# Where a gate's preparation, its placements and the first expert tile's transposes stand in an attention loop

## The chip, the cores and the metric

The kernel runs on one core of a Trainium2 chip. The metric is the time of one execution on the device in microseconds (us). The core has a matrix engine (TensorE, in rows PE, its weight loads PEld), a vector engine (VectorE, DVE), a scalar engine (ScalarE, ACT), a general engine (GpSimd, POOL) and SyncE (SP), which here only starts transfers. Each engine works off its own instructions in the order in which they are written, and waits for the others through semaphores. TensorE writes its results into PSUM, from which ScalarE and VectorE copy them away.

## What is computed

Three layers follow one another: a gated linear attention over 4 sequences of 768 rows with 8 heads of 48, a mixture of 8 experts (each row goes to the one expert with the largest logit), and a gated feed-forward layer. The inputs of the part that matters here are q, k, v, the forget logits f, the modality id of each row, the gate's weights and one bias per modality and expert.

```python
f = 1.0 / (1.0 + np.exp(-f_logit))
for t in range(S):
    state = f[:, :, t, :, None] * state + np.einsum('bhd,bhe->bhde', k[:, :, t], v[:, :, t])
    y[:, :, t] = np.einsum('bhd,bhde->bhe', q[:, :, t], state)
...
logits = x @ w_gate + modality_bias[modality_id]
e_idx = np.argmax(logits, axis=1)
for e in range(E):
    mask = e_idx == e
    h = np.maximum(x[mask] @ w1[e], 0.0)
    out[mask] = gate_w[mask, None] * (h @ w2[e])
...
return (silu * val @ w_out).astype(np.float32)
```

## The kernel before

**The loop.** The attention runs over 24 tiles of 128 rows (6 chunks of 4 sequences) in a pipeline of 32 steps, written out by hand in `attention_fast`; within `manual_schedule` each engine keeps the order of the text. A tile t passes p0 at step t-1, p1 at t+1, p2 at t+2, p3 at t+3 and p4 at t+4.

- p0: VectorE clamps f (line 104), ScalarE takes Exp and Ln and casts the high part lh, GpSimd subtracts for the low part ll (line 114).
- p1: TensorE forms the running sums cum (lines 123 and 124) in the PSUM tile pm. VectorE clamps them into bc (line 128), ScalarE makes em and ep, VectorE kp = k em (line 133), GpSimd qp = q ep (line 134). SP then copies the last row of ep into dd (line 137).
- p2: TensorE transposes kp into the PSUM bank pk and qp into pq (line 151); ScalarE copies them to kt and qt (line 153). Each bank holds one tile at a time.
- p3: TensorE multiplies kt and qt into pa (line 162), VectorE masks the result into am (line 165), in two halves.
- p4: TensorE adds the products of the state (line 175, from the second chunk on) and of am with v (line 177) in py; ScalarE copies py to xs. VectorE updates gm and the state (lines 182 to 196), TensorE forms the state's increment pu (line 187), GpSimd scales the state.

**The gate.** Tiles are gated in groups of 4, 4, 2, 3, 3, 2, 2, 1, 1, 1 and 1. A tile's xs is transposed at step t+5 (`early`, px on TensorE, xt on ScalarE) and multiplied with the gate's weights at t+6 (`logits`). At the last tile of a group, VectorE adds the bias (lg, line 413) and `route` finds the expert in five short operations at step t+6. `ranks` and `place` follow at step t+7: `place` has one operation per tile (line 472) and six more (lines 475 to 486), all on VectorE, and gives each row its place among its expert's rows. `send` writes one tile per step to DRAM (xo on ScalarE, an indirect transfer on GpSimd's queue). A step's order on the queues is: loads, p4, logits, ranks, p3, p2, early, place and route taking turns, p1, p0, share, send, and last what the expert layer has put into slot 2 of the step.

**The gate's preparation** (`Gate.fill`) is a generator in two parts. The first, at step 3, starts three loads on SP's queue: the weights, the biases and the modality ids (mi, line 368). The second, at step 5, has eight VectorE operations (lines 371 to 394), of which the first reads mi, and three GpSimd iotas. In the same step `Plan.setup` issues eleven more GpSimd instructions: nine iotas and two memsets.

**The first expert tile.** From step 17 on the loop also prepares the first tile of 512 rows of the expert with the most rows. `Experts.early` keeps a table of calls by step and slot; f there is 17. VectorE finds the expert at the end of step 17 (`plan.first`, lines 603 to 614). Gathers follow in steps 19 and 20 in slot 1, weight loads and their casts (line 758 on ScalarE, line 760 on VectorE) from step 18 on in slot 2. The rows are turned in steps 22, 23 and 24 (`turn`, slot 2): four transposes of TensorE into a borrowed PSUM bank (line 776), a cast xh on ScalarE (line 686) and a difference xl on VectorE (line 687). The bank is that of pq, so the next step's pq transposes wait until xl has read it. From step 25 on, TensorE multiplies for that tile between the last steps of the attention.

Of the kernel before, what the change touches and what calls it, by code (L numbers as in the profile page):

```python
# [7 lines left out]
F32 = mybir.dt.float32  # L8
# [9 lines left out]
P = 128  # L18
# [44 lines left out]
def attention_fast(tc, io, cst, ps, gate, plan, first):  # L63
    nc = tc.nc
    q, k, v, f = io
    ident, tri, mask4, onesc = cst["ident"], cst["tri"], cst["mask4"], cst["onesc"]
    gm = cst["gm"]
    with ExitStack() as ctx:
# [24 lines left out]
        def load(t, names="fkqv"):  # L93
            d = T.setdefault(t, {})
            for nm, a in zip("fkqv", (f, k, q, v)):
                if nm not in names:
                    continue
                x = ld.tile([P, H, D], F32, tag=nm, name=nm, bufs={"f": 3, "v": 7}.get(nm, 4))
                nc.sync.dma_start(x, src(a, t))
                d[nm] = x  # L100

        def p0(t):
            d = T[t]
            nc.vector.tensor_scalar_max(d["f"], d["f"], -LCLAMP)
            e = wk.tile([P, H * D], F32, tag="e", name="e")
            nc.scalar.activation(e, d["f"].rearrange("p h d -> p (h d)"), AF.Exp, scale=-1.0)
            nc.scalar.activation(e, e, AF.Ln, bias=onesc)
            if t == 0:
                d["l"] = e
                return  # L110
            lh = wk.tile([P, H * D], F32R, tag="lh", name="lh")
            nc.scalar.copy(lh, e)
            ll = wk.tile([P, H * D], F32R, tag="ll", name="ll")
            nc.gpsimd.tensor_tensor(out=ll, in0=e, in1=lh.bitcast(F32), op=ALU.subtract)
            d["l"] = lh, ll
# [84 lines left out]
        with tc.manual_schedule():  # L200
            for t, names in ((0, "fq"), (1, "f"), (0, "k"), (1, "q"), (1, "k"), (2, "f"), (0, "v"), (1, "v"), (2, "v")):
                load(t, names)
            p0(0)
            setup = gate.setup()
            for s in range(NTILE + 8):
                if s == 1:
                    blank()
                if s == 3:
                    next(setup)
                    nc.gpsimd.memset(sb, 0.0)  # L210
                if s == 5:
                    next(setup)
                    plan.setup()
                if s + 3 < NTILE:
                    load(s + 3, "f")
                if s + 2 < NTILE:
                    load(s + 2, "kqv" if s else "kq")
                first(s, 0)
                if 0 <= s - 4 < NTILE:
                    p4(s - 4)  # L220
                if s in TWICE:
                    gate.send(1)
                gate.logits(s - 6)
                gate.ranks(s - 7)
                first(s, 1)
                if 0 <= s - 3 < NTILE:
                    p3(s - 3)
                if 0 <= s - 2 < NTILE:
                    p2(s - 2)
                if 0 <= s - 5 < NTILE:  # L230
                    gate.early(s - 5, T.pop(s - 5)["xs"])
                gate.turns(gate.place(s - 7), gate.route(s - 6))
                if 0 <= s - 1 < NTILE:
                    p1(s - 1)
                if s + 1 < NTILE:
                    p0(s + 1)
                gate.share(s - 6)
                gate.send(1)
                first(s, 2)
            first(NTILE + 8, 0)  # L240
# [289 lines left out]
T1 = 512  # L530
# [159 lines left out]
class Experts:  # L690
# [18 lines left out]

    def lent(self, ps):  # L710

        self.pt = lambda: ps["q"].tile([P, T1], F32, tag="pq", name="pt")
        self.ph = lambda m: ps["ukq"[m % 3]].tile([P, T1], F32, tag="p" + "ukq"[m % 3], name="ph")

        def py():
            a = ps["a"].tile([P, 2, T1], F32, tag="pa", name="py")
            return [a[:, 0], a[:, 1], ps["y"].tile([P, T1], F32, tag="py", name="py2")]

        self.py = py
# [165 lines left out]
    def early(self, plan, ps, pm):  # L885

        d = {}
        w = [[] for _ in range(4)]
        h = {}

        def regs():
            plan.first(self.tc)
            d["e"] = self.pick(plan)

        def load(u):
            d["r", u] = self.load(d["e"], *divmod(u, 2))

        def halves(u):
            r = d.pop(("r", u), None)
            if r is None:  # L900
                w[u // 2].extend(next(d.pop(("h", u))))
            else:
                d["h", u] = self.halves(r, u % 2)
                next(d["h", u])

        def fetch():
            d["xr"] = self.xp.tile([P, T1 // P, RW], F32, tag="xr", name="xr", bufs=1)

        def gather(j):

            i = self.gather(plan.list0, d["xr"], j).ins
            self.tc.declare_no_dep(i, group=self.later, keep=d.setdefault("got", []), reason="no row of the list is among them")
            d["got"].append(i)
            self.tc.add_to_no_dep_group(self.later, i)

        def turn(kk):
            if kk == 0:
                d["x"] = self.split_x()
            self.turn(T1, d["xr"], d["x"], kk)

        def up(m):
            h[m] = self.up(T1, w[m // 2], d["x"], m)

        def down(m):
            if m == 0:
                d["py"] = self.py()
            self.down(T1, w[m // 2], h.pop(m), d["py"], m)

        def ahead():
            d["rg"] = self.regs(plan, 0)  # L930
            T, e, ids, off = d["rg"]
            xr = self.fetch(T, ids)
            d["w"] = [self.weights(e, 0), [], []]
            for u in (2, 3, 4):
                d["n", u] = self.load(e, *divmod(u, 2))
            d["next"] = xr

        def second():
            for u in (2, 3):
                d["w"][1].extend(list(self.halves(d.pop(("n", u)), u % 2))[1])  # L940
            d["n", 5] = self.load(d["rg"][1], 2, 1)
            T, _, _, off = d["rg"]
            self.note(T, d["next"], off)

        def last():
            x = d["x"] = self.split_x()
            pt = [ps["x"].tile([P, T1], F32, tag="px", name="pt"), ps["q"].tile([P, T1], F32, tag="pq", name="pt"), pm]
            for j in range(T1 // P):
                for kk in range(3):
                    self.flip(pt[kk], d["next"], j, kk)  # L950
            for kk in range(3):
                self.part(T1, pt[kk], x, kk)
            for u in (4, 5):
                d["w"][2].extend(list(self.halves(d.pop(("n", u)), u % 2))[1])
            d["rg1"] = self.regs(plan, 1)
            d["rows1"] = self.rows(*d["rg1"][0:1], *d["rg1"][2:4])

        self.lent(ps)
        at = {}

        def on(s, x, fn, *args):
            at.setdefault((s, x), []).append(lambda: fn(*args))

        f = FIRST + 8
        on(f, 2, regs)
        on(f + 1, 2, fetch)
        for j in range(T1 // P):
            on(f + 2 + j // 2, 1, gather, j)
        on(f + 4, 2, self.noted, d)
        for kk in range(3):  # L970
            on(f + 5 + kk, 2, turn, kk)
        for u in range(6):
            on(f + 1 + u, 2, load, u)
            on(f + 2 + u, 2, halves, u)
            on(f + 3 + u, 2, halves, u)
        n = NTILE
        for u in (6, 7):
            on(n + 3 * (u - 6), 2, load, u)
        made = plan.make(self.tc)
        for m in range(3):  # L980
            on(n + 1 + m, 2, up, m)
        on(n + 3, 2, halves, 6)
        on(n + 4, 2, halves, 6)
        on(n + 4, 0, down, 0)
        on(n + 5, 0, up, 3)
        on(n + 6, 0, down, 1)
        on(n + 6, 2, next, made)
        on(n + 8, 0, up, 4)
        on(n + 8, 0, down, 2)
        on(n + 8, 0, halves, 7)  # L990
        on(n + 8, 0, up, 5)
        on(n + 8, 0, halves, 7)
        on(n + 8, 0, down, 3)
        on(n + 8, 0, up, 6)
        on(n + 8, 0, ahead)
        on(n + 8, 0, down, 4)
        on(n + 8, 0, up, 7)
        for m in (5, 6):
            on(n + 8, 0, down, m)
        on(n + 8, 0, second)  # L1000
        on(n + 8, 0, down, 7)
        on(n + 8, 0, last)
        on(n + 8, 0, next, made)
        self.begun = d

        def run(s, x):
            for fn in at.get((s, x), ()):
                fn()

        return run  # L1010
# [442 lines left out]
```

## Time and profile before

| what | value |
|---|---|
| time, median of 3 runs | 904.59 us (903.18 to 910.25) |
| the profiled execution | 905.4 us |
| its span, first to last instruction | 903.7 us |
| TensorE busy | 863.8 us (96%) |
| VectorE busy | 489.8 us (54%) |
| ScalarE busy | 364.8 us (40%) |
| GpSimd busy | 203.3 us (22%) |
| mean granted clock of TensorE | 0.980 |

The span is cut into engines' busy times; matmuls are pipelined and their ends modelled, so a busy TensorE is not one at its peak. The granted clock is a share of the full 2.4 GHz; 0.50 is its lower level of 1.2 GHz. A row of a timeline gives a start, a duration, engine, line and operation, the tiles written and read, and in brackets how long the engine had been idle before and what ended it. Steps are not marked in the trace; a step is taken to begin with the first product of p4 on TensorE, and the other engines run up to some microseconds behind it.

### The profile page before, as it was taken

To read this page: it belongs to the slowest core of one execution; us is meant where nothing else is said; L and a number is where in the kernel's file an instruction comes from. 1 tells how busy PE (TensorE), PEld (TensorE's weight loads), DVE (VectorE), ACT (ScalarE), POOL (GpSimd) and SP (SyncE) were. 2 spreads that over 40 slices of the span, in tenths; PEclk is the share of its full clock that TensorE was granted. 3 is DMA by queue.
4 is the path that set the end of the run, shared out by engine and by line. 5 is a ranking of instruction groups with operands and counts; after the bars stand their busy time and mean duration, and the time that the engine had idled before them with its cause. 6 is when DMAs were issued, how large, how long until landed. Compare 5 with 4: busy or idle time off the path is not lost.

```text
span 903.7 us, 13025 instructions
## 1 busy us (share of the span) xinstructions
PE 863.8 (96%) x4778; PEld 748.0 (83%) x4778; DVE 489.8 (54%) x1030; ACT 364.8 (40%) x661; POOL 203.3 (22%) x245
## 2 busy tenths in 40 slices
PE   5899999899999999998999999999999999999993
PEld 4899999887787888777887888888888888888883
DVE  3466887657767557534999736227225422532220
ACT  6577777643454545423534412222131231122121
POOL 4346577523233232101312300010010010001001
PEclk9799999899999999999999999999999999999997
DMA  9857667214564464453223100000000000000001
GB/s 183 143 110 146 133 162 192 78 65 148 156 195 142 128 196 132 96 164 83 70 71 101 40 1 0 1 36 1 1 36 0 1 36 1 1 1 35 1 1 38
DMA packets 145291, 70.59 MB, mean 78 GB/s; under 512 B 113040, under 2 KB 140176, under 8 KB 145216
## 3 DMA queue, kind: packets, MB, share of 16 engines
q1 hardware_dynamic: 140320, 55.18, 24.7%
q0 software_dynamic: 4896, 14.47, 4.6%
q8 instruction: 40, 0.66, 0.3%
q14 instruction: 35, 0.29, 0.1%
HBM read 60.08 MB, written 9.52 MB: 77 GB/s over the span
## 4 chain that ended last, share of the span: by engine, by line
issue 33%; PE 10%; DVE 6%; POOL 2%; ACT 1%; DMA 1%; SPq 0%; POOLq 0%; ACTq 0%
PE po L1292 4%; PE pg L1271 3%; PE pv L1271 3%; POOL out_dram L1303 2%; DVE q L1122 1%; DVE t L1120 1%; DVE t L1121 1%; DVE h L1283 1%; DMA r<-in_moe_w_out_dram 1%; DVE sg L1280 1%; DVE t L1119 0%; DVE hl L687 0%; DVE h L1282 0%; DVE rr L1231 0%; SPq L1104 0%
## 5 line engine op out<-in xcount | busy, mean ns | idle before, releaser
L1278 DVE TENSOR_TENSOR h<-sg,pv 128x512 f32<-128x512 f32 x60 | 41.2, 687 | 192.0 <-PE pv L1271 192.0
L1303 POOL DMA_INDIRECT out_dram<-o,cid x24 | 23.3, 970 | 363.4 <-ACT o L1301 360.8
L1277 ACT ACTIVATE sg<-pg 128x512 f32<-128x512 f32 x60 | 35.9, 598 | 147.2 <-PE pg L1271 147.2
L686 ACT CAST hh<-h 128x512 fp32r<-128x512 f32 x70 | 43.4, 621 | 124.6 <-DVE h L1278 113.3
L1271 PE MATMUL pv<-xh,w1h 128*128 128x512 f32 x216 | 85.6, 396 | 2.1 <-DVE xh L1244 2.1
L1271 PE MATMUL pg<-xh,w0h 128*128 128x512 f32 x216 | 86.1, 398 | 0.3 <-DVE sg L1280 0.3
L1271 PE MATMUL pg<-xh,w0l 128*128 128x512 f32 x216 | 85.7, 397 | 0.0
L1271 PE MATMUL pg<-xl,w0h 128*128 128x512 f32 x216 | 85.4, 397 | 0.4 <-DVE xl L687 0.4
L1271 PE MATMUL pv<-xh,w1l 128*128 128x512 f32 x216 | 85.1, 394 | 0.2 <-POOL w1l L1125 0.2
L1271 PE MATMUL pv<-xl,w1h 128*128 128x512 f32 x216 | 85.1, 395 | 0.0
L687 DVE TENSOR_TENSOR hl<-h,hh 128x512 fp32r<-128x512 f32 x70 | 48.4, 693 | 33.5 <-ACT hh L686 33.5
L1292 PE MATMUL po<-w2h,hh 128*128 128x384 f32 x280 | 62.2, 340 | 2.2 <-ACT hh L686 2.1
L760 DVE TENSOR_TENSOR l<-r,h 128x768 fp32r<-128x768 f32 x48 | 46.1, 965 | 31.9 <-ACT h L758 31.5
L1292 PE MATMUL po<-w2l,hh 128*128 128x384 f32 x280 | 62.3, 341 | 0.0
L1292 PE MATMUL po<-w2h,hl 128*128 128x384 f32 x280 | 62.1, 340 | 0.0
L799 PE MATMUL ph<-xh,h 128*128 128x512 f32 x144 | 58.4, 406 | 0.6 <-ACT xh L686 0.6
L1292 PEld LDWEIGHTS po<-w2h,hh 128*128 128x128 f32 x280 | 50.9, 188 | 8.8 <-ACT hh L686 3.5
L177 PE MATMUL py<-v,am 128*128 128x48 f32 x384 | 55.3, 272 | 2.8 <-issue 2.7
L799 PE MATMUL ph<-xh,l 128*128 128x512 f32 x144 | 57.9, 402 | 0.0
L799 PE MATMUL ph<-xl,h 128*128 128x512 f32 x144 | 57.5, 400 | 0.2 <-DVE xl L687 0.2
L177 PEld LDWEIGHTS py<-v,am 128*128 128x128 f32 x384 | 51.7, 198 | 3.3 <-issue 3.0
L1292 PEld LDWEIGHTS po<-w2l,hh 128*128 128x128 f32 x280 | 50.7, 190 | 0.0
(302 smaller groups left out, 1848.4 us busy)
## 6 DMA issues: line engine op xcount, KB each, us to landing
r<-in_moe_w_dram SPq DMA_DIRECT2D x48, 384.0 KB
f<-in_f_logit_dram SPq DMA_DIRECT2D x24, 192.0 KB
q<-in_q_dram SPq DMA_DIRECT2D x24, 192.0 KB
k<-in_k_dram SPq DMA_DIRECT2D x24, 192.0 KB
v<-in_v_dram SPq DMA_DIRECT2D x24, 192.0 KB
r<-in_moe_w_gate_dram SPq DMA_DIRECT2D x12, 384.0 KB
r<-in_moe_w_val_dram SPq DMA_DIRECT2D x12, 384.0 KB
r<-in_moe_w_out_dram SPq DMA_DIRECT2D x12, 384.0 KB
```

The lines of the kernel that those rows point to most:

```text
L177: nc.tensor.matmul(py[:, h, :], d["am"][:, h % 2, h // 2, :], d["v"][:, h, :], start=(c == 0), stop=(c == 0 or h % 2 == 1))
L686: nc.scalar.copy(hi, src)
L687: nc.vector.tensor_tensor(out=lo, in0=src, in1=hi.bitcast(F32), op=ALU.subtract)
L760: self.nc.vector.tensor_tensor(out=l, in0=r, in1=h.bitcast(F32), op=ALU.subtract)
L799: nc.tensor.matmul(ph, a[:, kk, c], b[:, kk, 0:T], start=(n == 0), stop=(n == 8))
L1120: V.scalar_tensor_tensor(out=t, in0=top, scalar=-0x40000000, in1=t, op0=ALU.bitwise_and, op1=ALU.bitwise_or)
L1121: V.scalar_tensor_tensor(out=t, in0=low, scalar=29, in1=t, op0=ALU.logical_shift_right, op1=ALU.bitwise_or)
L1271: nc.tensor.matmul(p, a[:, kk, :], b[:, kk, :], start=(n == 0), stop=(n == 8))
L1277: nc.scalar.activation(sg, ps[0], AF.Silu)
L1278: nc.vector.tensor_tensor(out=h, in0=sg, in1=ps[1], op=ALU.mult)
L1292: self.nc.tensor.matmul(po[t], a[:, c], b[:, 0, :], start=(m == 0 and i == 0), stop=(m == self.KF - 1 and i == 2))
L1303: self.apart.add(nc.gpsimd.indirect_dma_start(out=self.out, out_offset=bass.IndirectOffsetOnAxis(ap=self.cid[:, i:i + 1], axis=0), in_=o, ...
```

## The change

Three things are moved. The second part of the gate's preparation comes at step 7 instead of 5, and the plan's setup at step 9. `place` no longer takes turns with `route` ahead of p1: `route` stays there, and `place` stands between p1 and p0. The turns of the first expert tile leave slot 2, the end of a step, for a new slot 3 between `early` and `route`, in the same steps 22, 23 and 24, and use the PSUM bank of pk instead of pq. Nothing is added to or taken from what is computed, and the number of instructions that work on data stays.

```diff
-                if s == 5:
+                if s == 7:
                     next(setup)
+                if s == 9:
                     plan.setup()
...
                     gate.early(s - 5, T.pop(s - 5)["xs"])
-                gate.turns(gate.place(s - 7), gate.route(s - 6))
+                first(s, 3)
+                gate.turns(gate.route(s - 6))
                 if 0 <= s - 1 < NTILE:
                     p1(s - 1)
+                gate.turns(gate.place(s - 7))
                 if s + 1 < NTILE:
                     p0(s + 1)
...
-        self.pt = lambda: ps["q"].tile([P, T1], F32, tag="pq", name="pt")
+        self.pt = lambda: ps["k"].tile([P, T1], F32, tag="pk", name="pt")
...
         for kk in range(3):
-            on(f + 5 + kk, 2, turn, kk)
+            on(f + 5 + kk, 3, turn, kk)
```

## Rows read from the trace of the kernel before

**Rows 1.** Waits over the span: engine, line, releaser: us in total, times, longest.

```profile
PE py L177 <- issue: 2.7, 1, 2.7
PE pq L151 <- DVE xl L687: 2.3, 1, 2.3
...
POOL qp L134 <- ACT ep L132: 47.4, 19, 7.8
```

**Rows 2.** Windows: stretch, length, busy us by engine, TensorE's clock, DMA share, GB/s.

```profile
23.10:31.44 8.34, 5.67 (x55) 5.16 (x54) 5.30 (x17) 5.30 (x10) 4.48 (x17) 0.97 0.74 102
31.44:42.17 10.73, 10.73 (x59) 10.40 (x60) 3.86 (x9) 4.30 (x8) 2.18 (x2) 0.55 0.90 174
42.17:48.22 6.05, 6.05 (x61) 5.91 (x60) 3.46 (x8) 4.81 (x10) 2.19 (x2) 1.00 0.63 123
...
155.45:167.06 11.61, 9.11 (x73) 8.27 (x72) 7.85 (x24) 6.83 (x13) 5.65 (x7) 0.87 0.21 70
167.06:175.59 8.53, 8.53 (x66) 7.97 (x66) 6.34 (x22) 5.37 (x11) 4.16 (x5) 0.78 0.29 93
...
190.76:198.50 7.74, 7.48 (x45) 6.63 (x44) 3.35 (x25) 2.69 (x7) 3.56 (x6) 0.78 0.15 55
```

**Rows 3.** Timelines of VectorE and GpSimd, steps 5 and 17: start, us, instruction.

```profile
27.28 1.00 POOL L114 TENSOR_TENSOR ll<-e,lh 128x384 fp32r<-128x384 f32 x1 [0.66 <-POOL qp L134]
27.50 0.82 DVE L371 CAST m<-mi 128x24 f32<-128x24 int32 x1 [2.16 <-DMA mi<-in_moe_modality_id_dram]
...
29.85 0.09 DVE L394 MEMSET countsa<- 128x40 f32 x1
...
121.70 2.35 DVE L609 SCALAR_TENSOR_TENSOR f_lim<-f_mx,f_pos 128x1 f32<-128x1 f32 x1
```

**Rows 4.** Timelines of VectorE and GpSimd, step 7.

```profile
44.06 0.35 DVE L104 TENSOR_SCALAR f<-f 128x384 f32<-128x384 f32 x1
44.45 1.19 POOL L134 TENSOR_TENSOR qp<-q,ep 128x384 f32<-128x384 f32 x1 [7.75 <-ACT ep L132]
46.60 1.00 POOL L114 TENSOR_TENSOR ll<-e,lh 128x384 fp32r<-128x384 f32 x1 [0.96 <-ACT lh L112]
46.72 1.29 DVE L165 TENSOR_TENSOR am<-pa,mask 128x512 f32<-128x512 f32 x2 [0.97 <-PE pa L162]
```

**Rows 5.** Timelines of ScalarE, VectorE, GpSimd and TensorE, steps 16 to 18.

```profile
112.52 0.50 ACT L525 COPY xt<-px 128x384 f32<-128x384 f32 x1
114.50 0.35 DVE L104 TENSOR_SCALAR f<-f 128x384 f32<-128x384 f32 x1
115.51 1.21 POOL L134 TENSOR_TENSOR qp<-q,ep 128x384 f32<-128x384 f32 x1
...
125.70 0.45 PE L123 MATMUL pm<-lh,tri 128*128 128x384 f32 x1 [0.62 <-DVE state L196]
```

**Rows 6.** Timelines of VectorE, GpSimd and TensorE, steps 19 to 21.

```profile
136.46 0.35 DVE L104 TENSOR_SCALAR f<-f 128x384 f32<-128x384 f32 x1
...
145.31 1.22 POOL L134 TENSOR_TENSOR qp<-q,ep 128x384 f32<-128x384 f32 x1
146.59 0.66 PE L151 MATMUL pq<-ident,qp 128*128 128x128 f32 x4
```

**Rows 7.** Timelines of VectorE, ScalarE and TensorE, steps 22 and 23.

```profile
158.08 0.56 DVE L128 TENSOR_SCALAR bc<-pm 128x384 f32<-128x384 f32 x1
159.70 0.35 DVE L104 TENSOR_SCALAR f<-f 128x384 f32<-128x384 f32 x1
160.15 0.53 ACT L106 ACTIVATE e<-f 128x384 f32<-128x384 f32 x1
163.73 0.83 PE L151 MATMUL pq<-ident,qp 128*128 128x128 f32 x4 [2.29 <-DVE xl L687]
163.86 0.59 ACT L153 COPY kt<-pk 128x512 f32<-128x512 f32 x1
```

**Rows 8.** Timeline of TensorE, step 29.

```profile
205.76 0.17 PE L458 MATMUL pm<-oh,tril 128*128 128x8 bf16 x1 [0.92 <-DVE lg L413]
```

## The prediction

> **What bounds the kernel now.** I read the waits of TensorE first. It is busy for 96% of the span, so only its waits, and its clock, can give time back. Two of its longest waits lie where the diff works: 2.7 us before the masked product of line 177, and 2.3 us before the transposes of line 151, which wait for VectorE's line 687 [rows 1]. The windows by step come second. A step begins with TensorE's first product of p4. Step 5 is 23.10 to 31.44 and ends with the first wait; step 6 then takes 10.73 us at a granted clock of 0.55, and step 7, with the same matmuls, 6.05 us at 1.00. Steps 23 and 24 (11.61 and 8.53 us) hold the second wait, at 0.87 and 0.78 [rows 2]. So each wait costs more than itself: the clock falls to its level of 1.2 GHz behind it. Third come the timelines of the other engines, to see what is late. In step 5 VectorE waits 2.16 us for the ids, and am, on which TensorE's next product waits, stands behind that [rows 3]. In step 23 ScalarE is late: it copies kt only at 163.86, and the first turn's split (xh, then xl of line 687) stood in its queue just ahead [rows 7].
>
> **The setup, two steps later.** The ids' load keeps its place in SP's queue; only the VectorE work behind it moves. The wait of 2.7 goes [rows 1], and so should the slow step behind it: 10.73 - 6.05 = 4.7 us [rows 2]. Together -7.4 us. What is late next: the eight VectorE operations, 2.4 us from 27.50 to 29.94 [rows 3], now stand in step 7 behind the clamp of f at 44.06, ahead of gm, state and am [rows 4]. In the old place 0.82 us went to the first of them, which ended 0.04 us after GpSimd's ll [rows 3]; in the new one qp (44.45) and ll (46.60) run beside them [rows 4]. am waited 0.97 us for TensorE there [rows 4], and that is the slack. Own work is about 2.4 - 0.8 + 0.2 = 1.8 us, so 1.8 - 1.0 = 0.8 is left, or nothing where gm and state would have waited too. With both GpSimd products in the way (0.9 of qp, 1.0 of ll) it is up to 1.9. I take 1.2: with the blocks am would start near 48.5 and end near 49.8, and the product wants its first half from 48.4 on. The three iotas of the gate move along. The plan's eleven GpSimd instructions go to step 9: at most 4.48 - 1.19 - 1.00 = 2.3 us there [rows 2 to 4]. I cost them at nothing: GpSimd waits 2.5 us on the mean, 19 times, before qp [rows 1], and the first user is step 17. Without that cover the scaling of the state would be late by those 2.3 us, with four steps until its next use.
>
> **The placement behind p1.** It came ahead of bc and now comes between kp and the clamp of f. bc, em, ep, kp and qp come earlier; the clamp, and with it ScalarE's Exp, Ln and lh and all that is queued behind them (xo, the weight cast, xs, kt, qt), does not. Two things make the clamp later than before: VectorE now idles while bc waits for TensorE, and the placement now runs beside GpSimd's qp. Operations of VectorE stop beside one: line 609, one column wide, took 2.35 us, to 124.05, where GpSimd's ll ended too [rows 3]. The Trainium skill (SBUF — State Buffer, Who interferes with whom) says that a VectorE instruction with two SBUF inputs contends with a GpSimd instruction that reads SBUF, and not with one that only writes. By that the iotas above block nothing, and the trace agrees so far: the block of 0.82 us ended with ll and not with the iotas behind it.
>
> Step 16 (two tiles placed): em is held by xt on ScalarE (112.52), so it starts near 112.9, kp ends near 114.1, the placement takes 1.4 us, and the clamp moves from 114.50 to about 115.5: +1.0 [rows 5]. From there to 125.70 GpSimd and ScalarE run nearly without a gap, and TensorE's cum already waits 0.62 us there [rows 5]: cost 1.0. Should the clamp fall behind qp, which begins at 115.51, it is 2.1 later. The earlier bc could give back the 0.62 instead. Ends -0.6 and 2.1; I take 1.0, the clamp's own shift.
>
> Step 19 (three tiles): the clamp moves from 136.46 to about 138.0, and qp at 145.31, behind the gathers in GpSimd's queue, by up to 1.0. The transposes of pq at 146.59 already follow qp's end (146.53) directly [rows 6], so they go along. Cost 0.8, ends 0 and 1.0. At steps 10 and 14 am keeps about a microsecond of slack as in rows 4: nothing. In steps 26 to 29 placement and routing no longer alternate; each such step's chain is some 0.8 us longer, hidden except where line 458 already waits 0.92 us behind VectorE [rows 8]: 0.4, ends 0 and 0.8.
>
> **The turn.** It uses pk's bank instead of pq's, and its new slot stands between early and route: earlier in program order than the old one, which closed the step. No queue entry is added. Step 22: the split now precedes bc, which starts near 156.5 instead of 158.08; kp ends at 158.2; the placement of three tiles starts, meets qp (158.5 to 159.7), and the clamp comes near 160.5 instead of 159.70: +0.8 [rows 7]. ScalarE's Exp moves to 160.9. Between Exp and kt lay 3.7 us [rows 7], now 3.2 since xh has gone: kt runs from 164.1 to 164.7. The pq transposes no longer wait. But the turn of step 23 writes pk's bank, so **TensorE now waits for kt**: the pq transposes could start at 163.73 - 2.29 = 161.44 [rows 7], they and px end their issue near 162.0, and the bank comes at 164.8, a wait of 2.8 us where 2.3 stood, but with less of the step behind it. With turn and cum at the lower clock (1.7 us) step 24 begins at 166.5, against 167.06: -0.6. At the upper clock both take 0.9 us, and with step 24 at full speed the gain is 0.6 + 0.8 + 8.53 x 0.22 = 3.3 [rows 2]. At the other end the clamp waits for ll as well, +1.0. I take -0.6.
>
> On the clock there is a choice. The stretch 190.76 to 198.50 ran at 0.78 though TensorE was idle for 7.74 - 7.48 = 0.26 us of it in all [rows 2]; so small matmuls can let the clock fall too, and I leave step 24 as it was. The Trainium skill (TensorE: Matmul & The Clock Gate, What's actually happening) has the clock fall when TensorE goes idle; by it alone step 24 would lie at full speed once its waits are gone, and the sum would be 1.9 us lower. The row speaks against it.
>
> **The sum:** -7.4 + 1.2 + 1.0 + 0.8 + 0.4 - 0.6 = -4.6 us. The profiled execution took 905.4 us (span 903.7), 0.8 above the median of 904.59. From step 30 on TensorE sets the pace (its later waits in the profile are single ones of at most 2.1 us that move along with it), so the gain is carried through. Predicted: 904.6 - 4.6 = **900.0 us**.
>
> **The rivals.**
> - Both waits vanish. The blocking by qp is slight, kt is copied in time, and the clock stays up. The setup gives 7.4, the turn 2.3 + 11.61 x 0.13 + 8.53 x 0.22 = 5.7, less 0.4: 891.9 us. For it: bc does come 1.6 us earlier in step 22. Against it: ScalarE's 3.2 us between Exp and kt. Chance 0.20.
> - Slower, by the placement in step 16. If the clamp falls behind qp (a margin of 0.03 us by my times), cum waits 0.62 + 2.1 = 2.7 us in step 18, as long as the wait that was followed by 4.7 us of slow clock; all else as forecast, the sum is -4.6 - 1.0 + 2.1 + 4.7 = +1.2: 905.8 us. It decides from a wait of some 2.3 us on, the shorter of the two that rows 1 show with a slow clock behind them. Chance 0.10.
> - The setup does not give what it says: the wait only moves to step 8 because its own 2.4 us and the blocking are the larger part, and a slow step follows it. Then 7.4 shrinks to 7.4 - 1.9 - 4.7 = 0.8, and the time is 904.6 - 0.8 + 1.6 = 905.4 us. Against it: 2.16 of the 2.7 were for the ids [rows 3]. Chance 0.08.
>
> **How the numbers follow.** The forecast has 0.62, with 896.5 to 903.5 as its own range. The range 891 to 905.5 reaches over the first rival and to the second. 1% of 904.6 is 9 us, about what a measurement tells from no change, so faster means under 895.5, slower over 913.6. Faster: rival one and a corner of the forecast, 0.22. Slower needs rivals two and three together: 0.03. Same: 0.75.
>
> **What would show it.** Right: no wait for the ids and about 6 us at a clock of 1.00 in step 6; a wait near 1 us before line 177 or 175 at step 8; a wait of TensorE for ScalarE's line 153 before the second turn; a longer wait at cum in step 18. Wrong: no wait at all around the turns, step 23 and 24 under 8 us each at full clock (rival one); or a clock under 0.7 over steps 8 or 18 (rivals two and three).

## The result, and the profile after

| | before | after |
|---|---|---|
| time, median (lowest to highest) | 904.50 us (902.23 to 911.10), 8 runs | 916.78 us (907.29 to 919.41), 8 runs |
| ratio, after to before | | 1.0116, 95% interval 1.0072 to 1.0160 |
| span of the profiled execution | 903.7 us | 917.5 us |
| mean granted clock of TensorE | 0.980 | 0.971 |

The change makes the kernel slower by 1.2%. The forecast was 900.0 us, range 891 to 905.5, with a chance of 0.03 for slower. The profile after is of one of four executions whose mean granted clock was 0.970 or 0.971. The other four had 0.979 to 0.984 and took 907.29 to 919.41 us; no trace shows where those lost their time.

First the waits of TensorE after (engine, tile and line, released by: us in total, times, longest):

```profile
PE py L175 <- ACT xs L179: 4.0, 4, 1.6
...
PE pt L779 <- ACT kt L153: 2.8, 1, 2.8
...
PE py L177 <- DVE am L165: 0.9, 2, 0.7
```

The waits of 2.7 and 2.3 us of [rows 1] are gone. Three others stand in their place, 7.7 us in all. That is only 2.7 us more than went; the other 11 of the span's 13.8 us are not in these waits. The windows by stretch have them (us, TensorE's busy time, instructions, granted clock, DMA share, GB/s). Before, steps 4 to 8, 9 to 16, 17 and 18, 19 to 21, 22 to 24, and the rest:

```profile
17.98:55.15 37.17, 34.50 (x289) 0.86 0.79 143
55.15:111.41 56.26, 56.13 (x544) 1.00 0.61 128
111.41:126.16 14.75, 14.13 (x135) 1.00 0.75 174
126.16:147.76 21.60, 21.30 (x204) 1.00 0.83 205
147.76:175.59 27.83, 25.33 (x210) 0.88 0.35 99
175.59:903.70 728.11, 704.44 (x3366) 0.99 0.20 62
```

After, the same six, and then steps 8, 18, 21, 23 and 24 by themselves:

```profile
18.47:52.64 34.17, 33.27 (x289) 0.90 0.81 147
52.64:110.28 57.64, 56.36 (x544) 1.00 0.62 129
110.28:130.81 20.53, 18.94 (x136) 0.75 0.67 153
130.81:157.72 26.91, 25.77 (x204) 0.82 0.71 171
157.72:188.73 31.01, 28.22 (x210) 0.78 0.20 64
188.73:917.50 728.77, 700.53 (x3365) 0.99 0.21 62
41.18:52.64 11.46, 10.56 (x68) 0.70 0.80 157
118.96:130.81 11.85, 11.85 (x68) 0.57 0.74 168
146.03:157.72 11.69, 11.69 (x67) 0.58 0.79 192
165.43:176.43 11.00, 8.21 (x72) 0.94 0.20 63
176.43:188.73 12.30, 12.30 (x66) 0.50 0.20 65
```

| stretch | forecast | measured |
|---|---|---|
| ahead of step 4 | 0 | +0.5 |
| steps 4 to 8 (setup) | -7.4 + 1.2 = -6.2 | -3.0 |
| steps 9 to 16 (placements of steps 10 and 14) | 0 | +1.4 |
| steps 17 and 18 (placement of step 16) | +1.0 | +5.8 |
| steps 19 to 21 (placement of step 19) | +0.8 | +5.3 |
| steps 22 to 24 (turn) | -0.6 | +3.2 |
| step 25 to the end | +0.4 | +0.7 |
| sum | -4.6 | +13.8 |

Four steps are slow at a clock of 0.50 to 0.70: 8, 18, 21 and 24, each behind one of the new waits, with the same matmuls that take about 7 us at 1.00. That is where most of the time went.

**Where the waits are made.** A row has the line number of its own kernel, and an edit shifts the lines below it: the placement's lines 472 to 486 of before are 475 to 489 here. Step 16 after, timelines of all engines:

```profile
113.61 1.93 DVE L483 TENSOR_TENSOR ps__1597<-ps__1597,oh 128x16 f32<-128x16 f32 x1
114.31 1.20 POOL L134 TENSOR_TENSOR qp<-q,ep 128x384 f32<-128x384 f32 x1
115.86 0.35 DVE L104 TENSOR_SCALAR f<-f 128x384 f32<-128x384 f32 x1
116.31 0.53 ACT L106 ACTIVATE e<-f 128x384 f32<-128x384 f32 x1 [3.23 <-DVE f L104]
118.45 0.46 ACT L179 COPY xs<-py 128x384 f32<-128x384 f32 x1
118.96 0.46 PE L175 MATMUL py<-state,qt 128*128 128x96 f32 x2 [1.59 <-ACT xs L179]
```

Read it downwards. A multiplication of the placement, 16 columns wide, takes 1.93 us because it meets GpSimd's qp; it ends where qp ends (115.5). The clamp of f stands behind it, ScalarE idles 3.23 us for the clamp, and everything in ScalarE's queue moves along: Exp, Ln, lh, xo and the copy of py. TensorE's next step needs py's bank and waits 1.59 us. The clamp comes 115.86 - 110.28 = 5.58 us after step 17 begins, where it was 114.50 - 111.41 = 3.09 [rows 5].

Step 19 after does the same:

```profile
139.69 1.59 DVE L475 TENSOR_TENSOR countsa<-countsa,rt 128x8 f32<-128x8 f32 x3
140.07 1.18 POOL L134 TENSOR_TENSOR qp<-q,ep 128x384 f32<-128x384 f32 x1 [0.94 <-ACT ep L132]
142.20 0.35 DVE L104 TENSOR_SCALAR f<-f 128x384 f32<-128x384 f32 x1
145.51 0.47 ACT L179 COPY xs<-py 128x384 f32<-128x384 f32 x1
146.03 0.46 PE L175 MATMUL py<-state,qt 128*128 128x96 f32 x2 [1.14 <-ACT xs L179]
```

In step 22 the late clamp makes kt late, and so the turn:

```profile
168.15 1.57 DVE L475 TENSOR_TENSOR countsa<-countsa,rt 128x8 f32<-128x8 f32 x3
171.09 0.53 ACT L106 ACTIVATE e<-f 128x384 f32<-128x384 f32 x1 [2.66 <-DVE f L104]
174.32 0.58 ACT L153 COPY kt<-pk 128x512 f32<-128x512 f32 x1
174.96 0.61 PE L779 MATMUL pt<-ident,xr 128*128 128x128 f32 x2 [2.79 <-ACT kt L153]
```

The setup in step 7 meets both of GpSimd's products, and am, behind it in VectorE's queue, is late at step 8 by 0.72 + 0.18 us:

```profile
37.45 1.19 POOL L134 TENSOR_TENSOR qp<-q,ep 128x384 f32<-128x384 f32 x1 [3.18 <-ACT ep L132]
37.50 1.17 DVE L376 TENSOR_SCALAR m<-m 128x24 f32<-128x24 f32 x1
39.61 1.00 POOL L114 TENSOR_TENSOR ll<-e,lh 128x384 fp32r<-128x384 f32 x1 [0.97 <-POOL qp L134]
39.79 0.97 DVE L396 TENSOR_TENSOR tril<-tri,ident 128x128 bf16<-128x128 f32 x1
...
42.26 0.42 PE L177 MATMUL py<-v,am 128*128 128x48 f32 x2 [0.72 <-DVE am L165]
```

### The profile page after: what moved, and what is told of

It is laid out like the page before. It is cut to its first block, busy times and chain, and to the rows that moved or that the text cites. A ratio compares the mean times of both kernels' runs of the same rounds, so it can differ in the third digit from the quotient of the medians.

```text
span 917.5 us, 13023 instructions
## 1 busy us (share of the span) xinstructions
PE 871.4 (95%) x4778; PEld 757.0 (83%) x4778; DVE 498.8 (54%) x1030; ACT 364.6 (40%) x661; POOL 202.4 (22%) x245
## 4 chain that ended last, share of the span: by engine, by line
issue 32%; PE 9%; DVE 6%; POOL 2%; DMA 1%; ACT 1%; SPq 0%; POOLq 0%; ACTq 0%
PE po L1295 3%; PE pv L1274 3%; PE pg L1274 3%; POOL out_dram L1306 2%; DVE q L1125 1%; DVE t L1123 1%; DVE t L1124 1%; DVE h L1286 1%; DMA r<-in_moe_w_out_dram 1%; DVE sg L1283 0%; DVE hl L690 0%; DVE t L1122 0%; DVE h L1285 0%; DVE rr L1234 0%; DMA out_dram<-o,cid 0%
## 5 line engine op out<-in xcount | busy, mean ns | idle before, releaser
L761 ACT CAST h<-r 128x768 fp32r<-128x768 f32 x48 | 39.7, 834 | 29.3 <-PE ph L802 12.2
```

Source lines behind the costliest of these rows:

```text
L761: self.nc.scalar.copy(h, r)
```

## The experiments

Ratios are to the kernel before on the same chip, as they were recorded, with a 95% interval. They are not the quotients of the two medians beside them: before's own runs scatter by 13 us within a group (899.8 to 913.1 where the median is 903.05). A median of before differs by some us between groups of runs, so times are compared within a group.

**1. Each part by itself.** The setup alone:

```diff
-                if s == 5:
+                if s == 7:
                     next(setup)
+                if s == 9:
                     plan.setup()
```

> The setup's move alone (VectorE's and GpSimd's part at step 7, the plan's at step 9), placement and turn as before. Theory A (in the changed kernel am was 0.90 us late at step 8, and the clock fell to 0.50 behind it until 52.2 us): steps 4 to 8 take 34.2 us in place of 37.2, with a wait near 0.9 us for am at step 8 and a stretch of half clock behind it; time before less 3.0, 901.5 us. Rival B (the prediction's own figure, 7.4 less 1.2): step 8 at full clock but for the wait, 898.3 us.

Measured: 897.51 us against 907.31, ratio 0.9923 (0.9878 to 0.9969). The trace has A's step 8, wait and slow clock:

```profile
40.91:52.37 11.46, 10.56 (x68) 0.70 0.87 168
145.17:169.09 23.92, 22.04 (x211) 1.00 0.35 98
```

The second row holds steps 22 to 24: 23.9 us, not the 27.8 of before, with the turn untouched. The wait of 2.3 us for xl is not there. It is absent too in the traces of experiments 3 (the setup in two parts) and 5 (in three), which keep the old turn, and in experiment 2 with the placement alone behind p0. It is there again in the two that move the placement alone to right behind p1 or inside it (2.35 and 2.25 us). So it hung on how the work ahead fell, not on the turn alone. That is how this version gains 0.8% though its step 8 is slow; its ten runs, 893.8 to 907.2, lie too far apart to tell A's 901.5 from B's 898.3 by time.

The placement alone:

```diff
-                gate.turns(gate.place(s - 7), gate.route(s - 6))
+                gate.turns(gate.route(s - 6))
                 if 0 <= s - 1 < NTILE:
                     p1(s - 1)
+                gate.turns(gate.place(s - 7))
```

> The placement behind p1 alone. Theory A (placement meets GpSimd's qp, the clamp behind it is about 2.5 us late in steps 16 and 19, ScalarE's copy of py follows it, and the clock falls behind the waits): waits for ScalarE's line 179 of about 0.6, 0.6, 1.6 and 1.1 us at steps 12, 16, 18 and 21, half clock behind the last two, +12 us: 916.5 us. Rival B (the prediction: 1.0 + 0.8 + 0.4, no slow clock): 906.7 us.

Measured: 920.01 us against 907.31, ratio 1.0166 (1.0107 to 1.0226), five runs. Theory A in the main. The waits for line 179 are 0.49, 0.98, 1.61 and 1.14 us; steps 18 and 21, behind the last two:

```profile
123.22:133.44 10.22, 10.22 (x68) 0.67 0.82 190
148.67:155.71 7.04, 7.04 (x67) 1.00 0.85 194
```

The half clock came behind the 1.61 but not, this time, behind the 1.14. Here the old turn's wait for xl is back (2.35 us), with 13.65 us of half clock behind it.

The turn alone:

```diff
-        self.pt = lambda: ps["q"].tile([P, T1], F32, tag="pq", name="pt")
+        self.pt = lambda: ps["k"].tile([P, T1], F32, tag="pk", name="pt")
...
+                first(s, 3)
...
-            on(f + 5 + kk, 2, turn, kk)
+            on(f + 5 + kk, 3, turn, kk)
```

> The turn's bank and slot alone. Theory A (the wait for kt, 2.8 us, takes the place of the one for xl, 2.3, and the slow stretch behind it is longer than the two before): steps 22 to 24 take 31.0 us in place of 27.8, 907.7 us. Rival B (the prediction): the wait is the same 2.8 us but the slow stretch is not longer, -0.6: 903.9 us.

Measured: 904.42 us against 907.31, ratio 0.9983 (0.9944 to 1.0021). Both theories' wait of 2.8 us is wrong here: steps 22 to 24 take 25.4 us at full clock, with two waits of about 1 us for kt.

```profile
156.41 0.66 PE L777 MATMUL pt<-ident,xr 128*128 128x128 f32 x4 [0.90 <-ACT kt L153]
...
166.04 0.66 PE L777 MATMUL pt<-ident,xr 128*128 128x128 f32 x4 [1.00 <-ACT kt L153]
```

So kt is 2.8 us late only where the placement stands behind p1. The three ratios add up to 1.0072; the rest to 1.0116 lies within the intervals, and this meeting of placement and turn is part of it.

**2. Is it the clamp?** The changed kernel with the placement behind p0, so that the clamp goes first; and the same with the placement moved alone:

```diff
-                gate.turns(gate.place(s - 7))
                 if s + 1 < NTILE:
                     p0(s + 1)
+                gate.turns(gate.place(s - 7))
```

> The changed kernel with the placement moved once more, behind p0, so that the clamp of f goes ahead of it on VectorE. Theory A (the late clamp makes the waits of steps 12, 16, 18 and 21): those four waits go, and the half clock behind two of them: the changed kernel less 12, 904.5 us. Rival C (what is late is the scatter on GpSimd, whose address the placement makes): the address is later still, the waits stay or grow, 916.8 us or more.

Measured: 899.70 us against 907.31, ratio 0.9924 (0.9888 to 0.9960). Theory A, and more than it asked for: no wait for line 179, and kt late by 0.30 us at the turn. The window is step 8:

```profile
41.18:49.45 8.27, 7.37 (x68) 1.00 0.85 166
```

This kernel's step 8 has the same instructions and the same waits for am, 0.72 and 0.18 us, as the changed kernel's (the row at 42.26 above stands in both traces), and took 8.27 us at full clock instead of 11.46. So behind a wait of 0.9 us the clock may fall or not, and here the fall cost 3.2 us.

> The placement alone, but behind p0 and so behind the clamp of f; setup and turn as before. Theory A (with the placement behind p1 alone, 1.017, nearly all of the loss is the clamp that is late): ratio 0.996 to 1.004, no wait for ScalarE's line 179. Rival B (a good part of the loss is that the addresses come later, whatever the clamp does): ratio over 1.008, with waits that lead to GpSimd's scatters.

Measured: 905.47 us against 903.05, ratio 0.9993 (0.9954 to 1.0031). Theory A. The placement is stretched no less (its copy of line 478 takes 2.88 us, across qp and ll), but now gm, the state and am stand behind it in place of the clamp, and am is 0.47 us late:

```profile
115.88 2.88 DVE L478 COPY countsa<-countsa 128x8 f32<-128x8 f32 x1
...
120.97 0.42 PE L177 MATMUL py<-v,am 128*128 128x48 f32 x2 [0.47 <-DVE am L165]
```

This kernel and that of the placement alone behind p1 differ in nothing but the order of the placement and p0, and p0 has only the clamp on VectorE. So what cost 1.7% was the clamp behind the placement.

**The stretch or the length?** The placement inside p1, ahead of kp:

```diff
+            if mid:
+                mid()
             nc.vector.tensor_tensor(out=kp[t % NB][:, :, 0:D], ...)
...
-                    p1(s - 1)
+                    p1(s - 1, lambda: gate.turns(gate.place(s - 7)))
```

> The placement alone, but inside p1, between the two exponentials and kp: still ahead of the clamp, but over before GpSimd's qp begins. Theory A (of the clamp's 2.5 us in step 16, 1.8 are line 483's block by qp, 1.93 us in place of 0.17): the clamp is at most 0.9 us late, the waits for line 179 stay under 0.6 us, no half clock behind them, ratio up to 1.005. Rival B (the placement's own 1.4 to 1.6 us ahead of the clamp are enough): waits of 1 us or more at steps 18 and 21, ratio 1.010 or more.

Measured: 911.72 us against 903.05, ratio 1.0068 (1.0031 to 1.0105), between the two theories. It does not decide, since the placement did not get out of the way. Two other operations of it were stretched:

```profile
114.87 1.55 DVE L476 TENSOR_TENSOR countsa<-countsa,rt 128x8 f32<-128x8 f32 x2
...
117.28 1.84 DVE L490 TENSOR_SCALAR pi<-pf 128x2 int32<-128x2 f32 x1
```

The first ran until GpSimd's scaling of the state ended (116.4), the second until qp did (119.1). Waits of 1.12 and 1.25 us followed ahead of steps 18 and 19, with half clock behind the second. How much the bare length would have cost stays open. Nor need all of the 1.0068 be the placement's: in this trace step 4 took 9.27 us, its matmuls at about twice their length, where the trace before has 5.12, and no tile is placed before step 10.

**3. The setup in two parts:**

```diff
                 if s == 5:
                     next(setup)     # iotas, memsets, tril: no ids needed
+                if s == 7:
+                    next(setup)     # the five operations on the ids
+                if s == 9:
                     plan.setup()
```

> The setup alone, but in two parts: what needs no ids (three iotas, two memsets, the tril subtraction) stays at step 5, the five VectorE operations on the ids come at step 7. Theory A (the 0.90 us at step 8 are the blocks of line 376 by qp, 1.17 in place of 0.20 us, and of line 396 by ll, 0.97 in place of 0.23, on top of the own work): without line 396 in step 7 am starts near 40.6 and step 8 has no wait; steps 4 to 8 take 29.7 us, in place of 37.2 before and 34.2 with the whole setup at step 7; ratio to before 0.991, and no run with a slow step 8. Rival B (the own work alone makes am late): a wait of 0.5 us or more stays.

Measured: 895.94 us against 903.22, ratio 0.9955 (0.9903 to 1.0006), five runs. B's wait stays, 0.51 + 0.17 us, and steps 4 to 8 take 31.2 us where A said 29.7; but the reason is A's: with line 396 gone, the next in the queue, gm, 4 columns wide, met ll in its place.

```profile
40.51 0.98 DVE L182 TENSOR_TENSOR gm<-gm,dd 128x4 f32<-128x4 f32 x1
```

**4. Another bank for the turn, and the bank alone:**

```diff
-        self.pt = lambda: ps["k"].tile([P, T1], F32, tag="pk", name="pt")
+        self.pt = lambda: ps["u"].tile([P, T1], F32, tag="pu", name="pt")
```

> The turn alone, in the new slot but in pu's bank in place of pk's. Theory A (in the new slot TensorE waits only for the copy out of the bank it shares with p2, kt: 0.9 and 1.0 us with the turn alone): no wait before a turn, steps 22 to 24 near 23.4 us in place of 27.8 before and 25.4 with pk; ratio 0.995. Rival B (the turn's split only moves the wait to the next user of the bank): TensorE waits for xl before line 187, 1 us or more.

Measured: 905.95 us against 903.22, ratio 1.0016 (0.9988 to 1.0043). Neither theory as a whole. There is no wait before a turn, as A said, and none for xl, but one for bc instead, since the turn's split stands ahead of bc in VectorE's queue. Steps 22 to 24 take 25.0 us, not A's 23.4:

```profile
160.29 0.81 PE L411 MATMUL pm<-wg,xt 128*128 128x8 f32 x6 [0.96 <-DVE bc L128]
```

> The turn alone, in pk's bank but in the old slot at the end of the step. Theory A (the split of the turn comes too late for the next user of the bank, and the transposes into pk come 0.5 us ahead of those into pq): a wait for xl of about 2.8 us before the pk transposes, ratio 1.000 to 1.003. Rival B (the bank alone is the cure): the wait goes, ratio 0.995.

Measured: 902.68 us against 903.22, ratio 1.0010 (0.9988 to 1.0031). The time is A's, the wait is not: 0.72 us, not 2.8.

```profile
163.74 0.66 PE L151 MATMUL pk<-ident,kp 128*128 128x128 f32 x4 [0.72 <-DVE xl L687]
```

None of the three places of the turn makes a difference that can be measured.

**5. A better version?** The setup in two parts, the turn in pu, the placement behind p0:

> The split setup, the turn in pu's bank and new slot, and the placement behind p0 (clamp first). Theory A (each wait goes where it is made): no wait over 0.6 us from step 4 to step 25; half clock only behind the waits for lg after step 25, if at all; ratio 0.987, some 12 us under before. Rival B (with the large waits gone the clock falls behind the small ones instead): stretches at 0.50 behind waits under 0.6 us, ratio 0.992 as with the clamp first alone.

Measured: 898.58 us against 903.22, ratio 0.9927 (0.9887 to 0.9967). It beats both kernels, by no more than the setup alone does. A's 0.987 is refuted. So is its "no wait over 0.6": 0.70 us before the second turn. B has the ratio but not the reason: in the trace the clock stayed at 1.00 from step 4 through step 25.

The setup in three parts, all else as before (no ids at step 5, the two small operations on them at step 6, the three wide ones at step 7):

```diff
-                if s == 5:
+                if s in (5, 6, 7):
                     next(setup)
+                if s == 9:
                     plan.setup()
```

> The setup alone in three parts: what needs no ids at step 5, the two small operations on the ids at step 6, the three 192 wide at step 7; the plan's at step 9. Theory A (an operation of VectorE that meets qp or ll is stretched to its end; with fewer of them in one step am is in time): the wait for am at step 8 under 0.3 us (0.68 with two parts, 0.90 with one), steps 4 to 8 near 30.2 us, ratio 0.990 to 0.993 and the least scatter of the setup's versions. Rival B (each added operation is stretched wherever it stands): waits for am of 0.5 us at steps 7 and 8 both.

Measured: 900.20 us against 903.05, ratio 0.9931 (0.9887 to 0.9976). No wait at all at step 8:

```profile
18.08:47.72 29.64, 29.64 (x290) 1.00 0.80 144
```

That is 7.5 us under before, about what the prediction had for the ids' wait and the slow step behind it (7.4), and TensorE kept the full clock from step 4 to step 24. But the twelve runs still scatter from 892.8 to 906.1, and A was wrong in that. The trace is of the run of 894.0 us, so it does not show what the longer runs lost. Four of the five runs above 903 us had a mean granted clock of 0.979 to 0.984, and all seven below 902 had 0.990 to 0.992; so half clock goes with most of it. Besides, the stretch from step 25 to the end takes 727.2 us in one trace (the placement alone behind p1) and 734.2 in another (the turn in pu). Where the half clock of the long runs lies is open. The versions that move the setup and keep the clamp ahead of the placement (0.9923 to 0.9955) can't be told apart.

**6. The changed kernel again.**

> The changed kernel once more, unedited, for a second trace. Theory A (the waits belong to the order of the program, the half clock behind them is not certain below some 1.5 us): the same waits at steps 8, 12, 16, 18 and 21 (0.90, 0.64, 0.64, 1.59, 1.14 us) and before the second turn (2.79), each within 0.1 us; half clock again behind the 1.59 and the 2.79, not necessarily behind the 0.90 and the 1.14. Rival B (the half clock comes at places of its own and makes the waits): the waits differ by more than 0.3 us where the clock differs.

Measured: 918.17 us against 902.70, ratio 1.0151 (1.0050 to 1.0251), two runs. Theory A's waits to 0.01 us, and the half clock again in all four steps, so that the second trace of the same program differs in neither:

```profile
42.51 0.42 PE L177 MATMUL py<-v,am 128*128 128x48 f32 x2 [0.72 <-DVE am L165]
...
119.20 0.46 PE L175 MATMUL py<-state,qt 128*128 128x96 f32 x2 [1.59 <-ACT xs L179]
...
175.20 1.02 PE L779 MATMUL pt<-ident,xr 128*128 128x128 f32 x4 [2.78 <-ACT kt L153]
```

## Why the prediction was wrong

- **The placement (+1.0 and +0.8) is the step that failed.** The two stretches grew by 5.8 and 5.3 us. Alone it costs 1.66%, 0.0166 x 907.3 = 15 us. In step 16 the prediction took the clamp's own shift, 1.0 us, and put "the clamp falls behind qp" aside as a rival with a chance of 0.10, though its margin was 0.03 us. It had said that the placement runs beside qp, and priced their meeting in step 22; but in step 16 it asked only whether the clamp would meet qp, not whether the eight short operations ahead of it would. One did, and the clamp came 2.5 us late, more than the end of 2.1. [rows 3] held the price: line 609, one column wide, 2.35 us.
- **The wrong queue was followed.** In step 19 the clamp moved by 1.5 us, as forecast (from 136.46 - 133.55 = 2.91 to 142.20 - 137.80 = 4.40 us after step 20 begins). The prediction followed it through GpSimd's gathers to qp and pq, and in step 16 to cum. What came last was ScalarE's copy of py, which it had named among "all that is queued behind them" and not priced: 1.59 and 1.14 us before the next step's first product, and 0.64 us twice for steps 10 and 14, which stood at nothing.
- **The clock.** The prediction let it fall from a wait of 2.3 us on, the shortest it had seen with a fall behind it; that was the shortest in one trace, not a bound. Waits of 0.90, 1.14 and 1.59 us had half clock behind them. Price of the fall alone: 11.46 - 8.27 = 3.2 us in step 8 (same waits, clamp first), 11.69 - 7.04 = 4.7 us in step 21 (same wait, placement alone). The Trainium skill (TensorE: Matmul & The Clock Gate, What's actually happening) says that the window in which activity is watched runs freely, so that where the clock changes depends on where in it the work falls; it says this of a kernel's first matmuls. That a pause within a kernel is likewise caught or missed by the moment is an inference: the two traces of step 8 fit it, as the same wait went either way, and the two traces of the changed kernel don't test it, as their falls lie in the same places.
- **The setup (-7.4 + 1.2).** The wait for the ids and the slow step 6 went, as said, and am was 0.90 us late where 1.2 was forecast. The -3.0 of the trace is short of -6.2 by the 3.2 us of half clock in step 8: the third rival, given 0.08. Both products were in the way, the case that the prediction had put at up to 1.9 us.
- **The turn (-0.6).** TensorE waited 2.79 us for kt where 2.8 was forecast, and step 23 became 0.6 us shorter, 11.00 against 11.61. Step 24, left as it was in the sum, ran wholly at 0.50: 12.30 us against 8.53. And the forecast's gain from the old wait for xl [rows 1] was a gain from one trace: versions that leave the turn alone lost that wait too.
- **Nothing for the plan's setup in step 9:** right. Steps 9 and 10 took 6.94 and 7.00 us.
- **0.4 from step 26 on:** near by luck. Everything behind step 24 is 0.7 us longer, but there TensorE's idle time grew from 728.11 - 704.44 = 23.7 to 728.77 - 700.53 = 28.2 us, while three stretches of half clock that the trace before has there (3.4 us each) are missing after. The wait behind VectorE's lg, from which the 0.4 were to come, grew by 0.2 us in all.
- **The chances.** The prediction said that slower needs rivals two and three together, which it gave 0.10 and 0.08, and put that at 0.03, as something rare. But they share both causes: a short VectorE operation that meets a GpSimd product, and a clock that falls behind less than 2.3 us. With the one true, the other was likely.

## What to carry to other kernels

Before moving short operations of one engine ahead of a critical one, look for what runs beside each of them, not beside the critical one only; and follow every queue behind it, to the copy that frees a PSUM bank. A wait on TensorE has to be priced with the slow clock behind it as a chance, even at 1 us. A wait seen in a single trace can belong to the way that work happened to fall, so what a change may give back from it is less than it shows.

## What was not expected of the hardware

- **How long a wait has half clock behind it.** Of TensorE's waits in steps 4 to 24 of the traces above: of 2.2 us and more, 11 of 11; of 1.6 us, 4 of 4; of 1.1 to 1.3 us, 3 of 5; of 0.9 to 1.05 us, 4 of 12; under 0.8 us, none. These are not independent draws: six of the eleven are the same wait, for the ids in step 5. One fall, in step 24 before, had no wait near it; and behind step 24, among the short matmuls of the routing, it fell behind 0.26 and 0.43 us in some traces and not in others.
- **Short VectorE operations with one input are stretched too.** A copy of one input took 2.88 us (line 478, eight columns), an operation with a constant 1.17 (line 376) and 1.84 (line 490), a product of two inputs 1.93 (line 483). The sentence that the prediction drew on speaks of two inputs only. The Trainium skill (SBUF — State Buffer, Who interferes with whom) also says that copies, casts and operations with a constant can take the ports that GpSimd uses, and these rows agree. Not every operation is stretched: in the trace before, a reduction (line 446, at 150.43) took 0.16 us within qp, and the two state products of line 194 (at 45.02), which read PSUM, took 0.72 us together within another. Lines 478, 483 and 490 had begun 0.6 to 0.7 us ahead of the recorded start of qp, while GpSimd still issued a scatter.
- **It goes the other way too.** With the turn in pu, a VectorE subtraction of 0.95 us that began 0.09 us ahead of qp kept its time, and qp took 1.93 us in place of 1.2:

```profile
161.48 0.95 DVE L761 TENSOR_TENSOR l<-r,h 128x768 fp32r<-128x768 f32 x1
161.57 1.93 POOL L134 TENSOR_TENSOR qp<-q,ep 128x384 f32<-128x384 f32 x1 [3.34 <-ACT ep L132]
```
